# A Fourier-mixing and gated-MLP block in float32: a rebuilt opening, and sequence results gathered in DRAM

## The chip, the core and the metric

The kernel runs on one core of a Trainium2 chip. The metric is the device time of one execution in microseconds (us). The engines are TensorE (PE), VectorE (DVE), ScalarE (ACT), GpSimd (POOL) and SyncE (SP). Each works through its own instructions in the order in which the program lists them; between engines only semaphores order the work. SP, ACT and POOL can each issue DMA transfers, and an issue stands in its engine's order like any other instruction.

## The reference

```python
def _A_ref(x, dft_seq_re, dft_seq_im, dft_hid_re, dft_hid_im):
    a = jnp.einsum("bsd,ed->bse", x, dft_hid_re)
    b = jnp.einsum("bsd,ed->bse", x, dft_hid_im)
    return jnp.einsum("ts,bse->bte", dft_seq_re, a) - jnp.einsum("ts,bse->bte", dft_seq_im, b)

def _B_ref(x, w1, w3, w2):
    h = _silu(jnp.einsum("bsd,df->bsf", x, w1)) * jnp.einsum("bsd,df->bsf", x, w3)
    return jnp.einsum("bsf,fd->bsd", h, w2)

mod = (_silu(c) @ w_mod).reshape(c.shape[0], 6, 1, -1)
sa, ca, ga, sb, cb, gb = (mod[:, i] for i in range(6))
h = _layernorm(x, axis=-1) * (1 + ca) + sa
x = x + ga * _A_ref(h, ...)
h = _layernorm(x, axis=-1) * (1 + cb) + sb
x = x + gb * _B_ref(h, w1, w3, w2)
```

All is float32, with S = 2048 rows, D = 512 columns and F = 1792 hidden columns of the MLP. Each product is made of three matmuls, since each operand is split into a rounded high part and the rest.

## The kernel before, in words

A big tile is 128 partitions by 2 by 512 numbers; 50 slots of SBUF hold such tiles, and `take` and `give` hand slots out and back. PSUM has eight banks of 128 x 512.

**The opening** (up to 93 us). The symmetry of the Fourier matrices folds the 16 row blocks of x into eight pairs, `k` = 0 to 7: a block of rows and its mirror image. For a pair the kernel loads x (`load_x`; for `k` of 4 and more the mirror half by an indirect DMA on POOL, a gather), takes the layer norm's statistics (`norm_stats`, `norm_root`, `norm_inverse`, `norm_scale`), turns the rows on PE (`turn_rows`), applies the modulation (`modulate_rows`), forms sums and differences of the two halves (`mirror_sums`, tile `hs`), splits them (`sum_highs` to `hh` on ACT, `sum_lows` to `hl` on DVE) and multiplies by the hidden Fourier weights (`hid_product`, `hid_difference`, `hid_mirror`). The results are split again into the operands `uh`, `us` and `ul` of the sequence products. The hidden weights come in four parts `dt`, split by `w_highs` and `w_lows`; `differ_w` makes their differences `wd` on POOL.

The modulation's first two columns come from `wmr`: `mod_scale` scales rows of the matrix by `silu(c)`, `mod_sum` adds them over the partitions by matmuls against a column of ones, and reads the sums at once into `mod1`. `keep_warm` issues matmuls on a tile of ones whose result nobody reads.

The order of the rest of the opening isn't written out: `task` names each piece, its needs, a rank and its duration on each engine that can do it, `at` gives the time at which loads are expected, and `arrange` (lines 1283 to 1302) takes, among the pieces that could begin within 0.3 us of the earliest, the one of the lowest rank, and emits it. `PACE` and `RANK` set the ranks. `check_w` squares parts of the weights for a later test of their symmetry.

**The sequence products** (93 to 270 us). For each half `j` of the output tiles and each `k`, `seq_unit` runs two units `m` (real and imaginary) of 24 matmuls over all eight banks: `x` for e = 0 to 3 (16 matmuls), then `y` (8). So there are 32 units; those of the second half are called u0 to u15 here. Operands are loaded by `load_some` (two plain loads on SP and two gathers on POOL for a unit) and prepared by `prepare_some`, four units ahead. At the middle of a half (`turn`, k = 3) the x banks, and at its end (`end`, k = 7) x and y, are read out: DVE adds them, times the gate `ga`, to the residual tiles `xr`, which `load_xt` has loaded; at the end ACT copies x to two tiles `sum`, and `add_sums` adds these later to two tiles `xr`, on DVE.

**The second layer norm** (`ln2(t)` for the four row tiles `t`, in pairs (0, 2) and (1, 3)) runs in the background. `step` puts a function into a queue with its cost on DVE and ACT and the slots it needs; after each unit of PE work, `advance(dve, act)` adds credit and takes steps from the queue as long as credit and slots last:

```python
while queue and len(free) >= queue[0][0] + kept():
    _, *cost, fn = queue[0]
    if any(us > 0 and credit[n] <= 0 for n, us in enumerate(cost)):
        return
    queue.popleft()
    if fn is None:
        return
```

A step without a function (`pause`) so ends the call. After a sequence unit a call brings 2.2 us of DVE credit, 5.0 once no operands are left to prepare; there is no call after the units (k, m) = (3, 0) and (7, 0). `ln2` goes: sums over rows (`a1`, `a1b`, `rows`, `partition_sums`), mean (`a2`), centering (`a3`), squares (`a3b`, ACT), `keep` (writes `xr` to DRAM, where the MLP's results are later added), sums of squares (`a4`, `a1b`, `rows`, `partition_sums`), root (`a6`, ACT), inverse (`a6b`), scaling (`a7`), modulation (`a8`, ACT); then `chunk_parts` splits the result into `h2h` (ACT) and `h2l` (DVE). `drain` takes steps regardless of credit until what it asks for has been emitted.

**The MLP** (from 270 us): `up(0, 0)`, `up(1, 0)` (four blocks of 12 matmuls each), eight `down` units of 6 matmuls, then `judge` (the test of the symmetry), then `up(0, 2)`, which drains until `h2h` and `h2l` of tile 2 are emitted. Each block or unit is followed by `beside`, which spends its credit on weight jobs first and, if none are left, on the background. A down unit's result goes to `y` on ACT, and POOL adds y to the sums in DRAM by an accumulating DMA (line 1119).

Of the kernel before, what the change touches and what calls it, by code (L numbers as in the profile page):

```python
# [42 lines left out]
def folded(nc, pools, c, cp, wmr, wmc, x, xt, ctr, cti, wdr, wdi, w1, w3, w2, out):  # L43
# [156 lines left out]
    def load_x(k):  # L200
# [12 lines left out]
    def load_wm(v):  # L213
        for k in range(2):
            wm[v, k] = take(F32, "wmr")
            nc.sync.dma_start(wm[v, k], wmr[v, k])
# [5 lines left out]
    def load_hid(dt):  # L222
        i, par = HD[dt]
        raw_w[dt] = take(F32, "w")
        for m, w in enumerate((wdr, wdi)):
            for q in range(2):
                nc.sync.dma_start(raw_w[dt][q * 64 : (q + 1) * 64, m, :], w[i][par::2, q])

    nc.sync.dma_start(cc, cp)
    load_x(0)  # L230
    load_wm(1)
    load_wm(0)
    load_hid(0)
    load_x(1)
    for dt in range(1, ND):
        load_hid(dt)
# [26 lines left out]
    )  # L263
    first_tmp = take(F32, "tmp")
# [4 lines left out]
    def keep_warm(count):  # L269

        for _ in range(count):
            nc.tensor.matmul(warm, onesf[:, :P], onesf, start=True, stop=True)
# [15 lines left out]
    mod_acc = bank(6)  # L288
# [11 lines left out]
    def mod_sum(v):  # L300

        for dt in range(ND):
            nc.tensor.matmul(
                mod_acc[:, v * ND + dt : v * ND + dt + 1],
                hid_cols(wm[v, 0][:, 0, :], dt),
                onesf[:, :1],
                start=True,
                stop=True,
            )
        nc.vector.tensor_scalar(  # L310
            mod1[:, v, :], mod_acc[:, v * ND : (v + 1) * ND], float(v), None, op0=OP.add
        )
# [79 lines left out]
    def differ_w(dt):  # L392
# [5 lines left out]
        def pool(out, a, b, op):  # L398
            nc.gpsimd.tensor_tensor(out=out, in0=a, in1=b, op=op)

        if HD[dt][1]:
            pool(dd[:, 0, :], r[:, 0, 1, :], r[:, 0, 0, :], OP.add)
            pool(r[:, 1, 1, :], r[:, 1, 1, :], r[:, 1, 0, :], OP.add)
            nc.gpsimd.tensor_scalar(dd[:, 1, :], r[:, 1, 1, :], -1.0, None, op0=OP.mult)
        else:
            pool(dd[:, 0, :], r[:, 0, 1, :], r[:, 0, 0, :], OP.subtract)
            pool(dd[:, 1, :], r[:, 1, 0, :], r[:, 1, 1, :], OP.subtract)
# [89 lines left out]
    def sum_highs(k):  # L497
        hh[k] = take(F32R, "hh")
        copy(flat(hh[k]), flat(hs[k]))

    def sum_lows(k):
        hl[k] = take(F32R, "hl")
        minus(flat(hl[k]), flat(hs[k]), flat(hh[k]).bitcast(F32))
        give(hs.pop(k))
# [19 lines left out]
    def hid_product(k, dt):  # L524
        if dt == 0:

            hb[k] = bank(4 + k % 2)
            nc.tensor.matmul(
                hb[k], nought, flat(wt[0])[:, :N], start=True, stop=False, skip_group_check=True
            )  # L530
        for m in range(2):
            for n, (a, b) in enumerate(PASSES):
# [28 lines left out]
    def hid_mirror(k, high):  # L561

        h1b[k, high] = to = bank(6 + high)
        u = h1[k].rearrange("p a (d n) -> p a d n", d=ND)
# [59 lines left out]

    zero = take(F32, "zero")
# [73 lines left out]
    def seq_unit(n, m, between=None):  # L699
# [52 lines left out]
        if turn:  # L752
            for e in range(ND):
                residual(j + 2, e, acc["x", e], ga2)
        if end:
            part = [take(F32, "sum") for _ in range(2)]
            for e in range(ND):
                copy(part[e // 2][:, e % 2, :], acc["x", e])
                residual(j + 2, e, acc["y", e], ga)
            for i in range(2):  # L760
                for t in (j, j + 2):
                    step(background, 0, lambda i=i, t=t: add_sums(t, i, part[i]), 1.3)
                step(background, 0, lambda i=i: give(part[i]))

    def add_sums(t, i, src):
        for q in range(2):
            residual(t, 2 * i + q, src[:, q, :], ga)

    xr = {}

    def load_xt(t):
        xr[t] = [take(F32, "xr") for _ in range(2)]
        for i in range(2):
            nc.sync.dma_start(xr[t][i], xt[t, i])

    def residual(t, e, src, gate):
        xs = xr[t][e // 2][:, e % 2, :]
        nc.vector.scalar_tensor_tensor(
            xs, src, gate[:, e : e + 1], xs, op0=OP.mult, op1=OP.add
        )  # L780

# [6 lines left out]
    xc, sums = {}, {}  # L788

    def ln2(t):  # L790
# [84 lines left out]
        def keep():  # L875

            for i in range(2):
                sums[t, i] = dram.tile([P, 2, N], F32, name=f"sum_{t}_{i}")
                nc.sync.dma_start(sums[t, i], xr[t][i])
                give(xr[t][i])  # L880
            xr.pop(t)
# [8 lines left out]
        for slots, fn, dve, act in (  # L890
            (2, a1, 1.2, 0.0),
# [183 lines left out]

    def load_sums(t):
        xr[t] = [take(F32, "xr") for _ in range(2)]
        for i in range(2):
            nc.sync.dma_start(xr[t][i], sums[t, i])
# [202 lines left out]

    def arrange(hand_over=0.1, window=0.3):
        while pending:
# [14 lines left out]
            _, name, _, fn, ways = pending.pop(at)  # L1299
            ends[name] = (begin + us, engine)  # L1300
# [7 lines left out]
    def last_steps(k):  # L1308
# [3 lines left out]
        task(f"up{k}", r + RANK["up"], [f"diff{k}", f"odd{k}"], lambda: high_columns(k, 0), DVE=0.61)  # L1312
        task(f"ush{k}", r + RANK["ush"], [f"up{k}"], lambda: high_columns(k, 1), ACT=0.55)
        task(f"ulh{k}", r + RANK["ulh"], [f"ush{k}"], lambda: high_columns(k, 2), DVE=0.61)

    PACE = 7.15
    RANK = {
        "stats": -17,
        "root": -15,
        "inverse": -12,  # L1320
        "scale": -11.5,
        "turn": -11,
        "mod": -7,
        "sum": -11.5,
        "hh": -6.5,
        "hl": -9.7,
        "h1": -5,
        "prod": -2,
        "odd": -3,
        "mirror": 3,  # L1330
        "uh": 4,
        "us": 5,
        "ul": 6,
        "diff": 3.4,
        "up": 6,
        "ush": 12,
        "ulh": 6.6,
# [10 lines left out]
    nc.gpsimd.memset(flat(zero), 0.0)  # L1348
# [11 lines left out]
    at(13.6, "mod")  # L1360
    at(12.0, "turn0.0", "turn0.1")
    at(14.0, "x1")
    for dt in range(ND):
        at((12.1, 16.0, 18.0, 20.0)[dt], f"w{dt}")
    for k in range(2, 4):
        at(22.0 + 2.0 * (k - 2), f"x{k}")
    for engine in clear:
        clear[engine] = 13.6
# [3 lines left out]
    for dt in range(ND):  # L1372
        task(f"wh{dt}", -8 + 2 * dt, [f"w{dt}"], lambda dt=dt: w_highs(dt), ACT=0.8)
        task(f"wl{dt}", -7 + 2 * dt, [f"wh{dt}"], lambda dt=dt: w_lows(dt), DVE=0.8)
        task(f"wd{dt}", -6 + 2 * dt, [f"wl{dt}"], lambda dt=dt: differ_w(dt), POOL=3.0)
    for dt in range(2):
        task(f"wn{dt}", dt, [f"wl{dt}"], lambda dt=dt: w_minus(dt), ACT=1.0)
# [1052 lines left out]
```

## Time and profile before

| | us |
|---|---|
| Runs | 714.74 median of 3 (714.67 to 715.85) |
| Span of the profiled execution, first to last instruction | 715.7 |
| of it: opening, to the first sequence product | 93.1 |
| sequence products | 177.1 |
| MLP, to the last matmul | 437.3 |

The span begins at the first instruction, 0.24 us in the trace's time, and ends after the last store. Lines of a timeline give start, duration, engine, source line, operation, out<-in tiles with their shapes, and how often; in brackets the idle time before, and what ended it. A duration is from issue to the end of the pipeline, so that neighbours overlap. In a table by stretches each engine has its busy time and, in brackets, its instructions, in the order PE, PE's weight loads, DVE, ACT, POOL; then come the granted clock of TensorE (1.00 is full), the share of the DMA engines and GB/s.

### The profile page before, as it was taken

How to read it: one execution, taken by the hardware profiler on the slowest of the kernel's cores; microseconds unless marked ns; L12 is line 12 of the kernel's file. 1: busy time of each engine (PE TensorE's matmuls, PEld its weight loads, DVE VectorE, ACT ScalarE, POOL GpSimd, SP SyncE). 2: the span in 40 equal slices, each digit the busy share in tenths (PEclk: the TensorE clock that was granted, in tenths of full speed). 3: DMA queues.
4: the chain of work that ended last, by engine and by line, in shares of the span. 5: the costliest groups of instructions: out<-in, count | busy, mean ns of one | idle time of the engine just before them, and what ended most of it. 6: DMA issues, size and time to landing. Idle time of an engine off the chain costs nothing.

```text
span 715.7 us, 8791 instructions
## 1 busy us (share of the span) xinstructions
PE 689.8 (96%) x3094; PEld 563.4 (79%) x3094; DVE 551.9 (77%) x873; ACT 428.7 (60%) x700; POOL 129.8 (18%) x147
## 2 busy tenths in 40 slices
PE   7699999999999999999999999999999999999995
PEld 3587888888888888777888788787788888888784
DVE  4889887999899977679997887897666456664663
ACT  4687975455453665646677767667665655656420
POOL 3520073443435000100100101011010101101000
PEclk8599999999999999999999999999999999999998
DMA  8630089878588530442667566376854748447503
GB/s 245 225 116 3 5 289 355 280 257 294 172 312 266 171 142 31 75 76 86 130 164 161 133 148 137 69 127 136 266 115 91 154 76 182 87 91 129 165 1 122
DMA packets 37956, 108.93 MB, mean 152 GB/s; under 512 B 4880, under 2 KB 5136, under 8 KB 37904
## 3 DMA queue, kind: packets, MB, share of 16 engines
q0 software_dynamic: 12352, 43.00, 28.8%
q1 hardware_dynamic: 25552, 65.29, 27.7%
q8 instruction: 26, 0.43, 0.2%
q14 instruction: 26, 0.21, 0.1%
HBM read 76.81 MB, written 33.55 MB: 154 GB/s over the span
## 4 chain that ended last, share of the span: by engine, by line
PE 60%; issue 23%; DVE 6%; DMA 4%; ACT 4%; POOL 2%; SPq 1%; POOLq 0%; ACTq 0%; DVEq 0%
PE bank L100 32%; PE bank L723 25%; POOL sum L1119 2%; PE bank L533 2%; DMA sum<-y 2%; DMA x<-in_x 1%; PE bank L569 1%; DMA wmr<-in_wmr 1%; DVE hl L90 1%; ACT hm L485 1%; PE bank L469 1%; DVE hs L90 1%; ACT y L317 0%; DVE hm L487 0%; ACT ho L87 0%
## 5 line engine op out<-in xcount | busy, mean ns | idle before, releaser
L100 PE MATMUL bank<-hf,w2h 128*128 128x512 f32 (+1 forms) x452 | 140.8, 391 | 1.0 <-ACT y L317 0.7
L1119 POOL DMA_DIRECT2D sum<-y x48 | 41.1, 856 | 390.9 <-ACT y L317 373.1
L100 PEld LDWEIGHTS bank<-hf,w2h 128*128 128x128 f32 x452 | 84.3, 188 | 22.8 <-DVE hf L90 3.4
L100 PE MATMUL bank<-hf,w2l 128*128 128x512 f32 (+1 forms) x226 | 87.6, 388 | 0.0
L317 ACT ACTIVATE y<-bank,gb 128x512 f32<-128x512 f32 x96 | 65.0, 683 | 19.1 <-PE bank L100 18.4
L87 ACT ACTIVATE hf<-v 128x512 fp32r<-128x512 f32 x56 | 35.3, 630 | 67.2 <-DVE v L96 62.6
L93 DVE TENSOR_TENSOR v<-bank,x 128x512 f32<-128x512 f32 x36 | 24.7, 686 | 34.8 <-PE bank L100 34.8
L170 POOL DMA_INDIRECT re<-in_ctr,mirror x32 | 36.5, 1142 | 73.8 <-PE bank L569 37.6
L723 PE MATMUL bank<-bh,us 128*128 128x512 f32 x128 | 49.9, 390 | 0.0
L723 PE MATMUL bank<-bh,ul 128*128 128x512 f32 x128 | 49.8, 389 | 0.0
L723 PE MATMUL bank<-d,us 128*128 128x512 f32 x128 | 49.8, 389 | 0.0
L723 PE MATMUL bank<-d,uh 128*128 128x512 f32 x128 | 49.8, 389 | 0.0
L723 PE MATMUL bank<-l,us 128*128 128x512 f32 x128 | 49.8, 389 | 0.0
L723 PE MATMUL bank<-l,uh 128*128 128x512 f32 x128 | 49.8, 389 | 0.0
L93 DVE TENSOR_TENSOR x<-bank,x 128x512 f32<-128x512 f32 x36 | 24.8, 688 | 32.4 <-PE bank L100 28.7
L100 PEld LDWEIGHTS bank<-hf,w2l 128*128 128x128 f32 x226 | 42.4, 188 | 8.4
L90 DVE TENSOR_TENSOR hf<-v,hf 128x512 fp32r<-128x512 f32 x56 | 38.5, 687 | 12.2 <-ACT hf L87 12.1
L1197 ACT ACTIVATE v<-v 128x512 f32<-128x512 f32 x36 | 22.8, 632 | 38.9 <-DVE v L93 38.9
L87 ACT ACTIVATE x<-bank 128x512 f32<-128x512 f32 x72 | 41.4, 587 | 7.1 <-PE bank L100 6.5
L170 POOL DMA_INDIRECT im<-in_cti,mirror x32 | 35.1, 1096 | 34.4 <-DVE l L90 9.7
L100 PE MATMUL bank<-h2h,w1h 128*128 128x512 f32 x80 | 31.8, 397 | 1.5 <-ACT h2h L87 1.5
L100 PE MATMUL bank<-h2l,w1h 128*128 128x512 f32 x80 | 32.0, 400 | 0.8 <-DVE h2l L90 0.8
(243 smaller groups left out, 1785.7 us busy)
## 6 DMA issues: line engine op xcount, KB each, us to landing
sum<-y POOLq DMA_DIRECT2D x48, 512.0 KB, 5.4
w<-in_w SPq DMA_DIRECT2D x42, 512.0 KB, 4.5
re<-in_ctr SPq DMA_DIRECT2D x32, 256.0 KB, 5.5
im<-in_cti SPq DMA_DIRECT2D x32, 256.0 KB, 4.9
wmc<-in_wmc SPq DMA_DIRECT2D x8, 512.0 KB, 6.9
xr<-in_xt SPq DMA_DIRECT2D x8, 512.0 KB, 7.6
sum<-xr SPq DMA_DIRECT2D x8, 512.0 KB, 6.6
x<-in_x SPq DMA_DIRECT2D x12, 256.0 KB, 4.5
```

The lines of the kernel that those rows point to most:

```text
L87: nc.scalar.activation(dst, src, AF.Copy, scale=scale)
L90: nc.vector.tensor_tensor(out=dst, in0=a, in1=b, op=OP.subtract)
L93: nc.vector.tensor_tensor(out=dst, in0=a, in1=b, op=OP.add)
L100: nc.tensor.matmul(acc, lhs[a], rhs[b], start=first and n == 0, stop=last and n == len(PASSES) - 1, skip_group_check=more,)
L170: nc.gpsimd.indirect_dma_start(dst, None, rows, bass.IndirectOffsetOnAxis(ap=at, axis=0))
L317: nc.scalar.activation(dst, src, AF.Identity, scale=by)
L469: nc.tensor.transpose(turned[k][dt // 2][:, at : at + P], hid_cols(xz[k][:, side, :], dt), anti if side and where(k)[1] else ident,)
L485: nc.scalar.activation(dst, src, AF.Identity, bias=sa, scale=ca1)
L533: nc.tensor.matmul(halves(hb[k])[:, m, :], sides((hh, hl)[a][k])[:, dt, m, :], wu[dt][:, b, m, :], start=False, stop=dt % 2 == 1 and n == ...
L723: nc.tensor.matmul(acc[what, e], lhs, rhs, start=begin and i == 0, stop=(end or (turn and what == "x")) and i == len(terms) - 1, skip_grou ...
L1119: nc.gpsimd.dma_start(sums[t, d // 2], y, accum_op=OP.add)
L1197: behind(k != 0 or q == 0, lambda: nc.scalar.activation(v, src, AF.Silu))
```

## The change

In the opening: part of the first loads are issued by ACT; the last `wmr` tile comes in two halves; the sums over partitions are 128 columns wide in banks of their own, and reading them is a step apart (`mod_read`); `hid_begin` and six narrow warming matmuls stand between; `differ_w` is on DVE; a gather of x waits, by a copy of one number on POOL, for `wd[0]`; pair 0's split and products go in halves; `arrange` fills PE's planned idle time with narrow warming matmuls until the first `hid_mirror`; ranks, durations and load times are new.

In the sequence products: `begin_sums` copies x from DRAM to the DRAM sums; `move` reads the banks out, times the gate, by ACT (at the end of the second half y by DVE) into tiles that POOL adds to the DRAM sums; `ln2` begins with `load_sums` and four pauses; `load_xt`, `residual`, `add_sums` and the store in `keep` go.

```diff
+    def load_x(k, other=nc.sync):
+        if k >= NK // 2:
+            nc.gpsimd.tensor_copy(held, wd[0][0:1, 1, 0:1].bitcast(F32))
...
-            nc.sync.dma_start(xz[k][:, 1, :], x[NK - 1 - i][1::2])
+            other.dma_start(xz[k][:, 1, :], x[NK - 1 - i][1::2])
...
+    def load_wm(v, k, queue):
+        wm[v, k] = take(F32, "wmr")
+        for n in range(2) if (v, k) == (0, 1) else (slice(0, 2),):
+            queue.dma_start(wm[v, k][:, n], wmr[v, k, :, n])
...
-    load_x(0)
-    load_wm(1)
-    load_wm(0)
-    load_hid(0)
+    load_x(0, nc.scalar)
+    load_wm(1, 0, nc.scalar)
+    load_wm(1, 1, nc.sync)
+    load_wm(0, 0, nc.scalar)
+    load_wm(0, 1, nc.sync)
+    for dt in range(2):
+        load_hid(dt, nc.sync)
     load_x(1)
...
-                mod_acc[:, v * ND + dt : v * ND + dt + 1],
+                mod_acc[v][:, cols(dt)],
                 hid_cols(wm[v, 0][:, 0, :], dt),
-                onesf[:, :1],
+                onesf[:, :P],
...
         if HD[dt][1]:
-            pool(dd[:, 0, :], r[:, 0, 1, :], r[:, 0, 0, :], OP.add)
...
+            plus(dd[:, 0, :], r[:, 0, 1, :], r[:, 0, 0, :])
+            nc.vector.scalar_tensor_tensor(
+                dd[:, 1, :], r[:, 1, 1, :], -1.0, r[:, 1, 0, :], op0=OP.mult, op1=OP.subtract
+            )
...
         if turn:
-            for e in range(ND):
-                residual(j + 2, e, acc["x", e], ga2)
+            move({(j + 2,): "x"}, ga2)
         if end:
...
+            move({(j, j + 2): "x", (j + 2,): "y"}, ga, j == 1)
...
+    def move(what, gate, both=False):
+
+        parts = {}
+        for i in range(2):
+            for to, name in what.items():
+                parts[to, i] = take(F32, "sum")
+            for q in range(2):
+                for to, name in what.items():
+                    dst, e = parts[to, i][:, q, :], 2 * i + q
+                    if both and name == "y":
+                        nc.vector.tensor_scalar(
+                            dst, acc[name, e], gate[:, e : e + 1], None, op0=OP.mult
+                        )
+                    else:
+                        copy_by(dst, acc[name, e], gate[:, e : e + 1])
+        for to in what:
             for i in range(2):
...
+                for t in to:
+                    nc.gpsimd.dma_start(sums[t, i], parts[to, i], accum_op=OP.add)
+                moved.append([3, parts[to, i]])
...
+    def begin_sums(t):
+        for i in range(2):
+            sums[t, i] = dram.tile([P, 2, N], F32, name=f"sum_{t}_{i}")
+            nc.sync.dma_start(sums[t, i], xt[t, i])
...
         for slots, fn, dve, act in (
+            (4, lambda: load_sums(t), 0.0, 0.0),
+            *[pause] * 4,
             (2, a1, 1.2, 0.0),
...
+            if engine == "PE" and filling:
+
+                keep_warm(max(0, int((begin - clear["PE"] - 0.1) / 0.23)), P)
...
-    PACE = 7.15
+    PACE = 7.39
...
-    for v in (1, 0):
-        for h in range(2):
-            mod_scale(v, h)
+    keep_warm(1)
+    for v, h in ((1, 0), (1, 1), (0, 0)):
+        mod_scale(v, h)
+    mod_sum(1)
+    copy(nought, zero[:, 0, :P])
     clear_z()
-    for v in (1, 0):
-        mod_sum(v)
-        keep_warm(2 if v else 1)
-    give(first_tmp)
...
+    hid_begin(0)
+    keep_warm(6, P)
+    mod_scale(0, 1)
+    mod_read(1)
+    mod_sum(0)
+    mod_read(0)
...
-        if k == 2:
-            load_xt(j + 2)
-        if k == 5:
-            load_xt(j)
+        if k == 1:
+            begin_sums(j + 2)
+        if k == 4:
+            begin_sums(j)
```

More of the change, by code (lines that the diff above doesn't have):

```diff
@@ L309, in mod_sum, with mod_read @@
             )
-        nc.vector.tensor_scalar(
-            mod1[:, v, :], mod_acc[:, v * ND : (v + 1) * ND], float(v), None, op0=OP.add
-        )
+    def mod_read(v):
+        for at in (slice(0, ND),) if v else [slice(dt, dt + 1) for dt in range(ND)]:
+            nc.vector.tensor_scalar(
+                mod1[:, v, at],
+                mod_acc[v][:, ::P][:, at],
+                float(v),
+                None,
+                op0=OP.add,
+            )
         for h in range(2):
@@ L522, in halves, with hid_begin, hid_product @@
         return b.rearrange("p (a n) -> p a n", a=2)
[L524 to L532, printed above, removed]
+    def hid_begin(k):
+        hb[k] = bank(4 + k % 2)
+        nc.tensor.matmul(
+            hb[k], nought, flat(wt[0] if k else zz)[:, :N], start=True, stop=False, skip_group_check=True
+        )
+    def hid_product(k, dt, ms=range(2), ns=range(3)):
+        if dt == 0 and k:
+            hid_begin(k)
+        for m in ms:
+            for n in ns:
+                a, b = PASSES[n]
                 nc.tensor.matmul(
@@ L772, in load_xt, with return_moved, load_sums @@
+    def return_moved():
+        for at in moved:
+            at[0] -= 1
+        while moved and moved[0][0] < 0:
+            give(moved.popleft()[1])
+    def begin_sums(t):
+        for i in range(2):
+            sums[t, i] = dram.tile([P, 2, N], F32, name=f"sum_{t}_{i}")
+            nc.sync.dma_start(sums[t, i], xt[t, i])
+    def load_sums(t):
         xr[t] = [take(F32, "xr") for _ in range(2)]
         for i in range(2):
[L774 to L780, printed above, removed]
+            nc.sync.dma_start(xr[t][i], sums[t, i])
@@ L875, in keep @@
         def keep():
[L877 to L881, printed above, removed]
+            for x in xr.pop(t):
+                give(x)
         def a9():
@@ L1504, in folded @@
     give(zz)
+    while moved:
+        behind(6, lambda t=moved.popleft()[1]: give(t))
     USED = {"w1": (0.0, 0.5), "w3": (1.2, 0.5), "y": (0.0, 0.6), "own": (0.7, 0.0)}
```

194 lines of the change are left out of this document (101 added, 93 removed).

## The prediction, made before the changed kernel was run

> **What bounds the kernel now.** The page comes first: the span, the engines' shares, the prices of a scaled copy on ACT and of an accumulating transfer.
>
> ```profile
> span 715.7 us, 8791 instructions
> PE 689.8 (96%) x3094; PEld 563.4 (79%) x3094; DVE 551.9 (77%) x873; ACT 428.7 (60%) x700; POOL 129.8 (18%) x147
> L317 ACT ACTIVATE y<-bank,gb 128x512 f32<-128x512 f32 x96 | 65.0, 683 | 19.1 <-PE bank L100 18.4
> L1119 POOL DMA_DIRECT2D sum<-y x48 | 41.1, 856 | 390.9 <-ACT y L317 373.1
> sum<-y POOLq DMA_DIRECT2D x48, 512.0 KB, 5.4
> ```
>
> TensorE is busy 96% of the span, so time is won or lost only where it idles or runs slowly. The busy time by stage (stretch, its length, then each engine's busy time) shows where that is.
>
> ```profile
> 13.30:18.80 5.50, 5.50 (x14) 3.43 (x15) 1.65 (x5) 0.83 (x2) 3.56 (x4) 0.50 0.98 246
> 18.80:36.00 17.20, 11.68 (x42) 9.23 (x42) 15.11 (x33) 12.73 (x24) 10.01 (x11) 0.50 0.69 222
> 36.00:40.00 4.00, 4.00 (x25) 3.54 (x24) 2.48 (x4) 3.12 (x8) 0.00 (x0) 0.99 0.00 0
> 40.00:93.10 53.10, 51.02 (x336) 45.06 (x335) 48.78 (x91) 44.79 (x90) 8.42 (x7) 1.00 0.19 56
> 93.10:270.20 177.10, 177.10 (x786) 146.69 (x785) 158.92 (x223) 95.72 (x185) 63.54 (x61) 1.00 0.75 252
> 302.90:310.00 7.10, 4.81 (x14) 3.54 (x14) 4.55 (x14) 4.41 (x6) 1.89 (x3) 0.76 1.01 181
> ```
>
> From 93.1 to 270.2 (the sequence products) TensorE never idles at full clock: nothing can be won there. The opening runs at half clock (0.50) up to 36 us. From 40 on three engines are near full at once: PE 96%, DVE 92%, ACT 84%. The other hole is the 7.1 us at 302.9. The timeline names the opening's events.
>
> ```profile
> 2.54 2.24 SPq L216 DMA_DIRECT2D wmr<-in_wmr  x4
> 13.22 1.54 DVE L296 SCALAR_TENSOR_TENSOR wmr<-wmr,sc,wmr 128x512 f32<-128x512 f32 x2 [0.79 <-DMA wmr<-in_wmr]
> 13.30 3.76 PE L272 MATMUL bank<-tmp 128*128 128x512 f32 x4
> 18.60 0.16 DVE L310 TENSOR_SCALAR mod<-bank 128x4 f32<-128x4 f32 x1 [3.77 <-PE bank L303]
> 18.80 0.54 DVE L487 TENSOR_SCALAR hm<-bank,mod 128x256 f32<-128x256 f32 x1
> 19.09 1.24 SPq L227 DMA_DIRECT2D w<-in_wdi  x2
> 24.07 0.80 PE L533 MATMUL bank<-wu,hh 128*128 128x256 f32 x2 [3.16 <-ACT hh L87]
> 93.08 0.40 PE L723 MATMUL bank<-bh,us 128*128 128x512 f32 x1
> ```
>
> The modulation sums could be read at about 15, but two warming calls (3.76 us) stand before them; hidden products begin at 24.07, sequence products at 93.08.
>
> **The opening.** Four edits have one answer: the earlier wm loads, the warming regrouped around wide column sums, `differ_w` moved from POOL to DVE, the new order. First the start. Three transfers fewer stand ahead of the last wm tile on SP (0.56 us of issue each), and it comes in two pieces; but all share the DMA engines, so I take 1.2 us off the 14.76 at which its scaling now ends and not 1.7, then add 0.7 for sums and reads: modulation starts at 14.3 instead of 18.80. Bounds: 13.3 if loads are quicker still, 18.8 if the six narrow warming matmuls delay the sums as the wide ones do.
>
> Then the work from there to 93.1. DVE has 15.11 + 2.48 + 48.78 = 66.4 us, ACT 12.73 + 3.12 + 44.79 = 60.6: 127.0 in 74.3 us, 85% of two engines. What changes in it:
>
> ```profile
> L399 POOL TENSOR_TENSOR wd<-w 128x256 fp32r<-128x256 f32 x6 | 5.8, 989 | 11.2 <-DMA w<-in_wdr 11.2
> L90 DVE TENSOR_TENSOR wu<-w,wu 128x256 fp32r<-128x256 f32 x2 | 1.4, 686 | 0.0
> L90 DVE TENSOR_TENSOR wu<-w,wu 128x256 fp32r<-128x256 f32 x2 | 0.8, 422 | 0.0
> L188 ACT ACTIVATE junk<-wd 128x512 f32<-128x512 f32 x4 | 2.6, 640 | 0.0
> ```
>
> The two `wu` rows are the same operation while POOL computes `wd` (19 to 27 us) and after (27 to 40). So `differ_w` on DVE adds 8 x 0.422 = 3.4 and ends an interference of 4 x 0.26 = 1.1 in these rows; the four checks (2.6) get ranks behind all else and fill gaps. 127.0 + 3.4 - 1.1 - 2.6 = 126.7, as before. At the old 85% it ends at 14.3 + 74.3 = 88.6, at 100% at 77.7. TensorE's floor is between: 11.68 at half clock is 5.8 at full, plus 4.0 and 51.0, 60.9; begun some 3 us after the modulation, 14.3 + 3 + 60.9 = 78.2. I take 92%, DVE's own share from 40 on, for both, because modulation and scaling may go to either: 126.7 / (2 x 0.92) = 68.9, so sequence products begin at 83.2: **-9.9 us** (ends: -4.5 and -13.5, the latter 1.4 above TensorE's floor). Held gathers and the split sums of block 0 are inside this term: the gathers wait for `wd` on POOL already, through its in-order queue.
>
> The clock needs a look. In 13.30 to 18.80 TensorE shows 5.50 of 5.50 busy, and the clock stays at 0.50 to 36. The Trainium skill (TensorE: Matmul & The Clock Gate, "What's actually happening") says that about 3.4 us of sustained activity releases a throttle that is the default. Row and rule disagree, unless the one-column sums in that stretch do not count as activity; the wide sums would then release the clock by about 18, which is the 92% case. By the row alone it stays at half to 36, which is the second rival.
>
> **Results taken out by ScalarE.** DVE loses 12 reads of banks and 16 additions over both halves, all under 100% TensorE: worth nothing. ACT gets eight copies at the end of the first half, in the order x0, y0, x1, y1. They can't pass y0, whose products end 1.4 us before the unit does (177.1 us for 32 units is 5.5 each, 0.23 for each of its 24 products, and six follow y0's); six copies of 0.683 later, 4.1, x3 is out, 2.7 us into the next unit, which reaches x3 after 2.7: 0 to 0.7, taken 0. POOL's eight accumulating DMAs (5.4 us to landing) stand ahead of gathers, behind operands prepared four units ahead: nothing.
>
> The Trainium skill (SBUF — State Buffer, "SBUF: two separate sides") says that a DMA issued from GpSimd can't have its descriptors written while DVE holds the shared port in a two-port mode. DVE is 90% busy here (158.92 of 177.10), so this speaks against the accumulation; by it each waits for one DVE operation, an estimate of 8 x 1.2 = 10 us over 90 us of POOL's queue, and the sum stays.
>
> **The second layer norm is what this costs.** Its background steps are spent by credit: a call after each sequence unit (u0 to u15 of the second half, none after u6 and u14), one after each of the eight up blocks (B1 to B8, from 270.2), one after each of eight down units (D1 to D8, from 291.98). A PAUSE ends its call. Before, tile 0 adds up to u4 and is done after u13; tile 2 follows at once:
>
> ```profile
> 262.24 1.22 DVE L93 TENSOR_TENSOR t<-xr,xr 128x1024 f32<-128x1024 f32 x1
> 288.48 0.69 DVE L93 TENSOR_TENSOR t<-t 128x512 f32<-128x512 f32 x1
> 291.87 0.25 DVE L813 TENSOR_REDUCE s<-q 32x16 f32<-32x64 f32 x1
> 294.92 0.31 ACT L853 ACTIVATE s<-s,eps 32x16 f32<-32x16 f32 x1
> 295.26 0.24 DVE L856 RECIPROCAL s<-s 32x16 f32<-32x16 f32 x1 [0.93 <-ACT s L853]
> 297.02 2.36 DVE L96 TENSOR_TENSOR xc<-xc,stat 128x1024 f32<-128x1024 f32 x2
> 298.33 1.52 ACT L867 ACTIVATE xc<-xc,sb,cb 128x512 f32<-128x512 f32 x2 [1.37 <-issue]
> 291.98 0.62 PE L100 MATMUL bank<-hf,w2h 128*128 128x512 f32 x2
> 302.63 0.39 PE L100 MATMUL bank<-hf,w2l 128*128 128x512 f32 x1
> 303.45 1.05 ACT L87 ACTIVATE h2h<-xc 128x1024 fp32r<-128x1024 f32 x1
> 304.56 0.50 PE L100 MATMUL bank<-h2h,w1h 128*128 128x512 f32 x1 [1.53 <-ACT h2h L87]
> 305.81 0.79 PE L100 MATMUL bank<-h2l,w1h 128*128 128x512 f32 x1 [0.76 <-DVE h2l L90]
> 309.95 0.39 PE L100 MATMUL bank<-h2h,w3h 128*128 128x512 f32 x1
> 307.58 0.42 DVE L979 TENSOR_REDUCE sq<-chk 128x8 f32<-128x256 f32 x1 [0.30 <-POOL sq L978]
> 310.54 0.14 DVE L999 TENSOR_SCALAR bad<-fine 1x1 int32<-1x1 f32 x1
> ```
>
> Tile 2 is barely ready when the third up block wants it: 1.53 us of wait, 0.76 more. After, the queue loses four steps of 1.3 and gets a load and four pauses for each tile. Tile 0's load is issued after u2, its first sum after u7 instead of u4; once nothing is left to prepare, calls bring 5.0 instead of 2.2, and its last low part comes after u15, with tile 2's load. Tile 2's pauses take u15, B1, B2, B3; then a1 after B4, a1b and rows B6, the sums B7, the mean B8, a3(0) D1, the squares D2 and D4, a4 D5, a1b D6, rows D7, the sums D8. That is where B7 stood before, at 291. The drain before the third up block emits all the rest at once.
>
> Times from there. D4 ends at 291.98 + 4 x 1.36 = 297.4; its copy and the second square (ACT in order, 0.7 + 1.05 and some queueing) end at 299.9; a4 1.2; a1b to sums 3.0 (288.48 to 292.12, less 0.6 of other work): 304.1, root 304.5. `judge` now stands ahead on DVE: 3.1 us (307.58 to 310.68), not before POOL is past the last accumulation at about 305: 308.1. Then reciprocal and spread 1.8, first product 1.2, the pairs on ACT 2 x 1.5, high part 1.05: 315.2 against 304.5 now, 10.7 later; a colder clock after it 0.7 more (from 305.81 to 309.95 the old stall takes 4.1 for 2.5 us of products). At u15 the low part of tile 0 falls behind the last bank reads on DVE: 0 to 1.2, taken 0.4. Together **+11.8** (8.3 without `judge`, 13.5 if POOL is later). ln2 of tiles 1 and 3 loses four additions and gains eight pauses that fall on idle calls; it meets its point at about 450 as before: 0.
>
> **Sum.** Span 715.7 - 9.9 + 11.8 = 717.6. The runs' median is 714.74 (714.67 to 715.85), 1.0 under the profiled span, so **716.6**, 0.3% slower. What a measurement of this kernel can tell from no change is 0.2%, 1.4 us.
>
> **Rivals.** *The opening wins more than the stall costs.* One mechanism: clock and vector engines hold 95% from 14.3 on, so sequence products begin at about 80 (-13.1) while the stall takes its lower end (+8.3): 709.9. It decides from the point where they begin before 81.3 (93.1 - 11.8). For it: PE, DVE and ACT reach 96, 92 and 84% from 40 on already. Against: weights are still being issued at 19 to 20 us, and three full engines wait for each other.
>
> *The clock stays at half in the lead-in*, 85% as before: -4.5 + 11.8, 722.0. For it: 5.5 busy us that released nothing. Against: the pieces that fill gaps.
>
> *POOL is late*: accumulations hold up gathers, and a sequence unit waits; six of 0.86 us behind eight copies of 0.68 hold the queue for 10.6 us. Against: four units (22 us) are prepared ahead. Held 25 us, by DMA engines that are 75% busy, the next unit is 3 late: 719.7.
>
> *The layer norm isn't late*, because DVE, relieved, catches up: 714.74 - 9.9 + 0.4 = 705.2. Against: the place in the order is given by calls, not by DVE's load.
>
> **How the numbers follow.** Forecast 0.48 (0.30 slower by over 0.2%, 0.15 within, 0.03 faster), opening wins 0.22, half clock 0.17, POOL 0.08, not late 0.05. Faster 0.03 + 0.22 + 0.05 = 0.30, same 0.15, slower 0.30 + 0.17 + 0.08 = 0.55. The forecast's own range is 713 to 720; taken to the first two rivals, 709.5 to 722.5, which leaves out the last and tails.
>
> **What would show it.** The first sequence product at 83 (80 to 89); clock 1.00 from about 18; `hm` at 14.3. In the PE waits one of about 11 us on `h2h` ahead of the third up block, `judge` ahead of the reciprocal. Sequence products still without a gap. Wrong would be a short wait there, or a start before 81.

## The result and the profile after

The changed kernel takes 728.62 us (median of 5 runs, 726.22 to 729.02) against 714.74 (714.39 to 715.85): a ratio of 1.018, 95% interval 1.0162 to 1.0198. It is 1.8% slower; the forecast was 716.6 us, 0.3% slower, with a range to 722.5. Both kernels were profiled once more later, and e1 (below) is the new opening alone. The stages of the five profiles, from the first matmul of each on TensorE's timeline:

| us | before (shown) | before again | after (shown) | after again | e1 |
|---|---|---|---|---|---|
| opening, to the first sequence product | 93.08 | 91.67 | 84.48 | 85.19 | 84.74 |
| sequence products | 177.14 | 177.15 | 182.55 | 184.17 | 177.10 |
| `up(0, 0)` to the start of the last down product | 32.41 | 32.41 | 33.72 | 33.73 | 32.41 |
| from there to `w3` of the third up block | 7.32 | 5.97 | 18.93 | 18.82 | 5.99 |
| rest | 405.75 | 405.70 | 404.72 | 404.59 | 404.76 |
| span | 715.7 | 712.9 | 724.4 | 726.5 | 705.0 |
| time of that execution | not known | 714.77 | 726.22 | 728.27 | 706.82 |

A run takes 1.7 to 2.4 us more than its span wherever both are known. So the profile shown of before is of an execution of some 717.5 us, an estimate; the fair base is the second one. Against it the changed kernel as shown gains 7.2 us in the opening and 1.0 in the rest, and loses 5.4 in the sequence products, 1.3 at the first up block and 13.0 at the third: 11.5 us. The second profile of after has the time of its session's median (728.27) and loses 7.0 in the sequence products.

The page of the profile after, first its shares, then its DMA issues (size of each, median us to landing):

```profile
span 724.4 us, 8924 instructions
PE 688.4 (95%) x3152; PEld 564.9 (78%) x3152; DVE 530.3 (73%) x849; ACT 438.7 (61%) x721; POOL 133.8 (18%) x157
sum<-y POOLq DMA_DIRECT2D x48, 512.0 KB, 5.4
re<-in_ctr SPq DMA_DIRECT2D x32, 256.0 KB, 7.7
sum<-sum POOLq DMA_DIRECT2D x16, 512.0 KB, 9.6
```

VectorE is relieved by 21.6 us (551.9 to 530.3) and nothing comes of it. The new accumulations take 9.6 us to land, not the 5.4 of the old ones. What TensorE waits for (in all, times, longest):

```profile
PE bank L100 <- ACT h2h L87: 12.6, 1, 12.6
PE bank L750 <- ACT sum L335: 3.6, 1, 3.6
PE bank L100 <- DVE h2l L90: 1.5, 2, 1.0
```

The first row is the forecast's; the second wasn't forecast. Its story begins 45 us earlier, on POOL, at the end of the first half. The timeline of after:

```profile
173.92 1.91 POOL L805 DMA_DIRECT2D sum<-sum  x2 [7.82 <-ACT sum L335]
176.22 1.73 POOL L805 DMA_DIRECT2D sum<-sum  x2 [0.39 <-ACT sum L335]
184.42 0.85 POOL L805 DMA_DIRECT2D sum<-sum  x1 [6.47 <-DMA sum<-sum]
191.33 0.85 POOL L805 DMA_DIRECT2D sum<-sum  x1 [6.05 <-issue]
192.48 1.08 POOL L170 DMA_INDIRECT re<-in_ctr,mirror  x1 [0.30 <-issue]
202.55 0.69 DVE L90 TENSOR_TENSOR l<-re 128x512 fp32r<-128x512 f32 x1 [11.89 <-DMA re<-in_ctr,mirror]
204.90 0.63 ACT L188 ACTIVATE re<-l 128x512 f32<-128x512 f32 x1 [15.70 <-DVE d L93]
221.85 2.40 ACT L335 ACTIVATE sum<-bank,ga 128x512 f32<-128x512 f32 x4
222.57 0.50 PE L750 MATMUL bank<-bh,us 128*128 128x512 f32 x1 [3.56 <-ACT sum L335]
```

POOL issues four accumulations of x, then stops: the accumulation of y goes into a tile of DRAM that one of x is still being added to, and waits for it, 6.47 us. The next one waits 6.05; its row names no releaser, but the trace fits the same cause: the two accumulations of x into these two tiles land at 184.14 and 190.83, 0.3 and 0.5 us before y's are issued. The next gather is issued at 192.48, 14.5 us after the last of x, its operand reaches VectorE after 11.89 us of idleness, and ScalarE after 15.70. The four units prepared ahead are used up; from then on preparation trails, until at the turn of the second half ScalarE takes the banks out only at 221.85, behind a square of an operand for the test of the symmetry, and TensorE stands 3.56 us and then runs at half clock for a while. Busy time by stretch:

```profile
174.00:200.00 26.00, 26.00 (x116) 21.55 (x115) 12.02 (x15) 10.10 (x21) 11.14 (x12) 1.00 0.99 246
222.00:232.00 10.00, 9.43 (x34) 7.58 (x35) 8.82 (x13) 6.41 (x13) 6.88 (x7) 0.83 1.03 270
16.20:84.50 68.30, 64.78 (x444) 58.63 (x444) 63.69 (x131) 63.88 (x131) 13.01 (x15) 1.00 0.34 101
```

While POOL stands still TensorE notices nothing (26.00 of 26.00): the loss appears at 219, some 40 us after POOL's first wait began. From 222 the clock is at 0.83 over ten us, worth 1.7; with the 3.56 that is 5.3 of the 5.4. The third row answers to the opening's forecast.

The third up block went as the prediction's row of steps said:

```profile
297.55 1.23 DVE L93 TENSOR_TENSOR t<-sq,sq 128x1024 f32<-128x1024 f32 x1 [2.09 <-ACT sq L884]
303.18 0.31 ACT L892 ACTIVATE s<-s,eps 32x16 f32<-32x16 f32 x1
303.74 0.42 DVE L1017 TENSOR_REDUCE sq<-chk 128x8 f32<-128x256 f32 x1 [1.76 <-POOL sq L1016]
306.76 0.23 DVE L895 RECIPROCAL s<-s 32x16 f32<-32x16 f32 x1
312.66 1.99 ACT L87 ACTIVATE h2h<-xc 128x1024 fp32r<-128x1024 f32 x2
313.75 0.80 PE L100 MATMUL bank<-h2h,w1h 128*128 128x512 f32 x1 [12.61 <-ACT h2h L87]
319.68 0.39 PE L100 MATMUL bank<-h2h,w3h 128*128 128x512 f32 x1
```

The squares are added at 297.55, the root is at 303.18, the test (`judge`, L1017) stands ahead of the reciprocal, and the first product comes at 313.75.

### The profile page after: what moved, and what is told of

Same layout as the page of the kernel before. It is cut to its first block, busy times and chain, and to the rows that moved or that the text cites. A ratio compares the mean times of both kernels' runs of the same rounds, so it can differ in the third digit from the quotient of the medians.

```text
span 724.4 us, 8924 instructions
## 1 busy us (share of the span) xinstructions
PE 688.4 (95%) x3152; PEld 564.9 (78%) x3152; DVE 530.3 (73%) x849; ACT 438.7 (61%) x721; POOL 133.8 (18%) x157
## 4 chain that ended last, share of the span: by engine, by line
PE 63%; issue 11%; DVE 8%; DMA 8%; ACT 6%; POOL 2%; SPq 1%; POOLq 0%; ACTq 0%; DVEq 0%
PE bank L100 47%; PE bank L750 12%; DMA sum<-sum 3%; DMA im<-in_cti,mirror 2%; PE bank L559 1%; DMA wmr<-in_wmr 1%; PE bank L598 1%; DMA sum<-y 1%; ACT xc L906 1%; POOL im L170 1%; DVE xc L96 1%; POOL re L170 1%; SPq L231 1%; ACT hf L87 1%; PE bank L576 1%
## 5 line engine op out<-in xcount | busy, mean ns | idle before, releaser
L335 ACT ACTIVATE y<-bank,gb 128x512 f32<-128x512 f32 x96 | 65.4, 684 | 21.6 <-PE bank L100 21.4
L1230 ACT ACTIVATE v<-v 128x512 f32<-128x512 f32 x36 | 22.8, 632 | 35.6 <-DVE v L93 35.6
L100 PE MATMUL bank<-h2h,w1h 128*128 128x512 f32 x80 | 32.3, 403 | 12.6 <-ACT h2h L87 12.6
L170 POOL DMA_INDIRECT im<-in_cti,mirror x32 | 33.0, 1031 | 23.7 <-issue 6.7
```

Of the source, the lines that this page charges most:

```text
L100: nc.tensor.matmul(acc, lhs[a], rhs[b], start=first and n == 0, stop=last and n == len(PASSES) - 1, skip_group_check=more,)
L170: nc.gpsimd.indirect_dma_start(dst, None, rows, bass.IndirectOffsetOnAxis(ap=at, axis=0))
L335: nc.scalar.activation(dst, src, AF.Identity, scale=by)
L1230: behind(k != 0 or q == 0, lambda: nc.scalar.activation(v, src, AF.Silu))
```

## The experiments

**One part alone.** e1 undoes the change in the sequence products (old `residual`, `add_sums`, `load_xt`, `keep`, no pauses); e2 undoes the opening.

> The new opening with the old way of taking out the sequence results. Theory 'POOL is late' (the sequence products lost 5.4 us, in the profile of the changed kernel, to accumulating DMAs in front of the gathers): none are there now, so the sequence products take 177 us again, the third up block waits 1.5 us as before, and the time is 714.7 - 8.6 = 706 us. Rival 'the new opening hands operands over late': the sequence products still take 182 us, 711 us. If the opening's gain is given back later, 714.

Measured: 708.13 us against 716.44 of before in the same session, ratio 0.9892 (0.9869 to 0.9916). Opening 84.74, sequence products 177.10, the third up block as before. The opening alone is a gain of 1.1%, and in this profile it gives nothing back (others do lose something at the start of the sequence products, see "After again").

> The old opening with the new way of taking out the sequence results. If the two parts add up: sequence products 182 us, 12.6 us of wait before the third up block, 728.6 + 8.6 = 737 us. Rival (the loss in the sequence stage comes from both together): sequence products 177 us, 727 us.

Measured: 735.06 us, ratio 1.0269 (1.0238 to 1.0299); opening 92.49, sequence products 181.92, 13.4 us of wait before the third up block. The parts add up roughly: -8.3 and +18.6 make +10.3, against +12.6 to 13.9 for both. The loss comes with the results' new way.

**The accumulations.** e3 issues the same transfers, two of them later:

```diff
-        for to in what:
+        for to, name in what.items():
             for i in range(2):
-                for t in to:
-                    nc.gpsimd.dma_start(sums[t, i], parts[to, i], accum_op=OP.add)
-                moved.append([3, parts[to, i]])
+                if name == "y" and not both:
+                    put_later.append([4, lambda to=to, i=i: put(to, i)])
+                else:
+                    put(to, i)
```

> The changed kernel, but the two accumulating DMAs of y at the end of the first half are issued four units later, behind the gathers. The same transfers and the same bytes. Theory 'POOL is late': the waits of 6.5 and 6.0 us on POOL ahead of the gathers go, VectorE's wait of 11.9 us goes, the sequence products take 177 to 178 us: 728.6 - 5 = 723 us. Rival 'the DMA engines are full' (share 1.05 at 186 to 200 us): the gathers land as late as before, sequence products 182 us, 728 us.

Measured: 722.39 us, 1.009 (1.0067 to 1.0114), 6.2 us below the changed kernel; sequence products 177.61. The timeline of e3:

```profile
176.60 1.73 POOL L804 DMA_DIRECT2D sum<-sum  x2 [0.39 <-ACT sum L335]
178.63 1.08 POOL L170 DMA_INDIRECT re<-in_ctr,mirror  x1 [0.30 <-DMA re<-in_ctr]
192.59 0.94 POOL L170 DMA_INDIRECT im<-in_cti,mirror  x1 [2.21 <-issue]
193.53 1.93 POOL L804 DMA_DIRECT2D sum<-sum  x2
193.09 0.69 DVE L90 TENSOR_TENSOR l<-re 128x512 fp32r<-128x512 f32 x1 [2.06 <-DMA re<-in_ctr,mirror]
194.22 1.23 DVE L93 TENSOR_TENSOR d<-re,re 128x1024 fp32r<-128x1024 f32 x1 [0.45 <-DMA re<-in_ctr,mirror]
```

The first gather goes out at 178.63, right behind the accumulations of x; eight are issued before y's two, which now find their predecessors landed and go in 1.93 us without a wait. VectorE idles 2.06 us where it idled 11.89. The bytes are the same, so it was the order on POOL and not the DMA engines. The rule that the prediction cited from the Trainium skill (SBUF — State Buffer, "SBUF: two separate sides") is about a two-port mode of VectorE. VectorE works at 193.09 and 194.22 and the two issues run through; but no row shows that these two operations hold the port in such a mode, so the rule isn't tested here, and a VectorE that is 90% busy was no measure of it.

**The layer norm.** e4 takes tile 2's pauses away by loading earlier, and e6 moves the test:

```diff
+            *[(4, lambda: load_sums(t), 0.0, 0.0), *[pause] * 4] * (t != PAIRS[0][1]),
...
             (0, keep, 0.0, 0.0),
+            *[(4, lambda: load_sums(2), 0.0, 0.0)] * (t == PAIRS[0][0]),
```

> The changed kernel, but the load of tile 2's sums is issued with tile 0's steps and tile 2 has no pauses of its own. Theory 'the pauses push the second layer norm of tile 2 behind': the wait before the third up block falls from 12.6 us to between 0 and 2, the time to 728.6 - 11.5 = 717 us. Rival 'the steps are late through VectorE or ScalarE, not through the calls': the wait stays above 8 us, 725 us.

Measured: 721.32 us, 1.0085 (1.0055 to 1.0114). That is 7.3 us less, not 11.5. The third block's stage falls from 18.93 to 12.25: 4.5 us of wait on `h2h` are left, and then 2.4 on `h2l`, for now the test stands ahead of `h2l`. Tile 0 is still three units later than before, and so is all behind it.

```diff
-    judge()
     up(0, 2)
+    judge()
```

> The changed kernel, but the test of the symmetry is moved behind the third pair of up blocks. The forecast put 3.1 us of the wait before that block down to it (reciprocal behind the test on VectorE): the wait on h2h falls from 12.6 to 9.5 us, 728.6 - 3.1 = 725.5 us. Rival: the test only fills time in which VectorE would wait for the root (303.49) anyway: 728 us.

Measured: 725.65 us, 1.0146 (1.0119 to 1.0172); the wait on `h2h` is 9.4 us. The test's 3.1 us were sized rightly, but half of it comes back in the trace: the test now stands among the pair sums on VectorE, and behind the block TensorE waits 1.9 us, 0.5 before, for a bank that ScalarE copies.

> The changed kernel with three mends: the accumulating DMAs of y four units later (as in e3), tile 2's load without pauses of its own (as in e4), and the test of the symmetry behind the third pair of up blocks, not ahead of it. If the losses are those two and add up: 728.6 - 6.2 - 7.3 - 2.4 (the wait on h2l that e4 still had behind the test) = 712.7 us. Rival 'the results by ScalarE cost nothing in themselves': then 708, as with the new opening alone. Rival 'the mends get in each other's way': above 716.

Measured: 717.34 us, 1.0037 (1.0019 to 1.0056). Expected too low: against e1 the profile still loses 5.0 us at the third up block, 1.7 behind it (the test again), 1.6 in the sequence products and 1.3 at the first up block.

e11 gives tile 0 two pauses in place of four, so that its first sum stands after u4 as before; the test is where it was.

> The changed kernel with the accumulating DMAs of y four units later (e3), tile 2's load with tile 0's steps (e4), and two pauses in place of four behind tile 0's load, so that tile 0's first sum comes after u4 as before. Theory 'the layer norm is late by calls alone': the wait before the third up block is 1.5 us as before, from the last down unit to the block's w3 6 us in place of 18.9, the whole 709 to 710 us, 1 to 2 above e1. Rival 'VectorE or ScalarE is late for its own reasons': the wait of 4.5 us of e4 stays, 714 us.

Measured: 719.69 us, 1.0059 (1.0042 to 1.0076). The half of it on the layer norm is right to the hundredth: 5.97 us to the third `w3`, as in before again, 32.42 to the last down product. But the sequence products take 188.39. The timeline of e11:

```profile
190.98 2.04 SPq L834 DMA_DIRECT2D xr<-sum  x2
213.82 1.23 DVE L93 TENSOR_TENSOR t<-xr,xr 128x1024 f32<-128x1024 f32 x1 [5.22 <-DMA xr<-sum]
228.90 0.80 PE L750 MATMUL bank<-bh,us 128*128 128x512 f32 x1 [7.74 <-ACT sum L335]
```

The load is issued at 190.98 and is there at 213.8. The sum that needs it stands in VectorE's order among the preparations of operands and holds them for 5.22 us; TensorE pays 7.74 at the same place as after, and a cold clock behind it. So the pauses are no oversight: they cover the way back from DRAM, which before didn't exist. With them the layer norm is late, without them the operands are.

**The opening's parts**, each undone in e1. e7 leaves out the narrow matmuls that `arrange` puts into planned idle time; e8 computes the differences of the weights on POOL; e14 has the old `PACE` and `RANK`; e15 has no `held` copies.

> e1 (new opening alone, 708.1 us, first sequence product at 84.7) without the 50 and more narrow warming matmuls that fill TensorE's planned idle time. Theory 'the fillers hold the clock': TensorE is idle from 16.2 to 22.2, the clock falls to 0.50 there and comes back only after some us of unbroken work; the first sequence product is at 87 to 89, 711 us. Rival 'the wide sums release it and that is enough, VectorE and ScalarE set the pace': 84.7, 708 us.

> e1 with the differences of the hidden weights back on POOL (in the planner too). The forecast counted 3.4 us more on VectorE and 1.1 us less interference for the move to VectorE; by that, undoing it gives 2.3 us of VectorE's time back: the first sequence product at 83.5, 707 us. Rival 'POOL's 12 us of differences and the gathers behind them are late': 86 to 88, 710 us.

> e1 (708.1 us, first sequence product at 84.7) with the old PACE and RANK, all else of the opening new. If the searched order is what raises the use of VectorE and ScalarE from 85 to 92%: first sequence product at 88, 711 us or more. Rival 'the differences on VectorE (4.7 us, e8) and the fillers (2.2 us, e7) are all of it': 85 to 86, 709 us.

> e1 without the copies on POOL that hold the gathers of x until the weights' first difference is there. If holding keeps the DMA engines (share 1.0 and more until 17 us) free for the weights: without it four gathers of 256 KB go out from about 10 us, the weights come some 3 us later, first sequence product at 86 to 88, 710 us. Rival 'the hold does nothing': 84.7, 708 us.

| | us | ratio (95%) | first sequence product |
|---|---|---|---|
| e1 | 708.13 | 0.9892 (0.9869 to 0.9916) | 84.74 |
| e7, no fillers | 712.28 | 0.9956 (0.9942 to 0.997) | 86.92 |
| e8, differences on POOL | 713.2 | 0.9968 (0.9951 to 0.9986) | 89.41 |
| e14, old order | 712.65 | 0.9964 (0.9946 to 0.9982) | 88.33 |
| e15, gathers not held | 712.26 | 0.9949 (0.9933 to 0.9965) | 87.74 |

Each part alone is worth 4 us or more; 2.2 + 4.7 + 3.6 + 3.0 exceeds the whole gain, so they hang together: with one of them undone the order no longer fits the rest. e8's expectation was wrong in sign; POOL takes 1.9 to 3.1 us for each of the four differences, one after the other until 22.9, and that these are on the way to the operands is likely but not shown. In e15 the four gathers stand ahead of the weights, and the modulation begins late. Its first row in the timeline of e15:

```profile
18.95 1.02 ACT L499 ACTIVATE hm<-bank,mod 128x256 f32<-128x256 f32 x2 [1.22 <-DVE mod L322]
```

And in that of e1, 2.5 us earlier:

```profile
16.41 1.02 ACT L501 ACTIVATE hm<-bank,mod 128x256 f32<-128x256 f32 x2 [1.89 <-DVE mod L324]
```

**The clock.** e9 puts wide sums into the kernel before; e10 is the kernel before itself.

> The kernel before with one thing changed: the modulation's sums are 128 columns wide in two banks of their own, in place of one column. In the profile of before TensorE is busy without a break from 11.82 to 20.9 us and the clock stays at 0.50 until 36. Theory 'one-column matmuls do not count as activity': with wide sums in their place the clock is back at 1.00 by 19 us; the lead-in's hidden products are at full speed, but it drops again in the idle time after 20.9, so the first sequence product is only 0 to 3 us earlier (90 to 93), 712 to 715 us. Rival 'the clock does not see the width': 0.50 until 36 as before, 93.1, 715 us.

> The kernel before, unchanged. The forecast took the runs to be 1.0 us under the profiled span (714.74 against 715.7). In the changed kernel the runs are 1.8 to 2.2 us over their spans. If that is so here too, the span of this profile is about 713, and the profile shown of before was of one of the slower executions; which stage is shorter shows where executions differ. Rival: span 715.7 and time 714.7 again.

e9: 714.34 us, 0.9977 (0.9964 to 0.9991), first sequence product at 91.07. It doesn't decide: the clock was at 1.00 there until 20 us, so nothing was to be released. e10: 715.42 us, span 712.9 in a run of 714.77: the profile shown of before was one of the slower executions, as was expected. Its opening is 1.4 us longer and its third up block too, and the clock is what differs. The stretches in which it changes (the last three figures are clock, DMA share and GB/s), first in the profile shown of before:

```profile
12.00:12.25 0.25, 0.25 (x4) 0.25 (x4) 0.25 (x1) 0.25 (x1) 0.00 (x0) 0.81 1.02 238
36.00:37.00 1.00, 1.00 (x6) 0.84 (x5) 0.98 (x1) 0.44 (x2) 0.00 (x0) 0.98 0.00 0
```

In before again, with two stretches between the changes:

```profile
9.00:12.00 3.00, 1.80 (x8) 1.43 (x8) 1.93 (x3) 2.45 (x5) 0.00 (x0) 0.56 1.05 348
12.77:16.18 3.41, 3.41 (x10) 2.38 (x11) 2.21 (x4) 0.83 (x2) 2.01 (x3) 0.50 1.08 257
16.18:19.59 3.41, 3.41 (x11) 2.38 (x11) 0.16 (x1) 0.00 (x0) 1.92 (x4) 0.50 0.98 246
28.00:30.00 2.00, 2.00 (x12) 2.00 (x11) 1.93 (x7) 0.87 (x2) 1.70 (x2) 0.54 0.97 381
```

In e7:

```profile
19.00:20.00 1.00, 0.00 (x0) 0.00 (x0) 0.96 (x4) 1.00 (x3) 0.00 (x0) 0.97 0.88 221
26.00:28.00 2.00, 2.00 (x10) 1.64 (x9) 1.97 (x4) 0.37 (x1) 1.84 (x2) 0.81 0.75 281
```

In e1:

```profile
9.25:9.50 0.25, 0.25 (x3) 0.25 (x3) 0.00 (x0) 0.25 (x1) 0.00 (x0) 0.72 1.03 393
12.75:13.00 0.25, 0.25 (x4) 0.25 (x3) 0.21 (x2) 0.00 (x0) 0.00 (x0) 0.96 1.13 279
```

A mean of 0.81 over 0.25 us is 0.62 of it at 1.00: so the clock falls at 12.16 in before and comes back at 36.04, at 9.36 and 29.84 in before again, at 19.94 and 26.76 in e7, at 9.36 and 12.77 in e1. The clock was low for 23.88, 20.48, 6.82 and 3.41 us: 7, 6, 2 and 1 times 3.41. The Trainium skill (TensorE: Matmul & The Clock Gate, "What's actually happening") gives a free-running window of 3413 ns, whose place differs from run to run; these rows agree. In e7 TensorE is idle from 15.8 to 21.83 for want of fillers and pays two windows at half clock. What runs in the two windows from 12.77 of before again, in which it never idles, is in its timeline:

```profile
12.38 1.87 PE L303 MATMUL bank<-tmp,wmr 128*128 128x1 f32 x8 [1.54 <-DVE wmr L296]
14.11 3.76 PE L272 MATMUL bank<-tmp 128*128 128x512 f32 x4
17.67 1.71 PE L303 MATMUL bank<-tmp,wmr 128*128 128x1 f32 x8
```

Each has some 1.3 to 1.7 us of one-column matmuls in it.

**After again.**

> The changed kernel, unchanged. Its profiled run took 726.22 us, the median 728.62: 2.4 us lie in no stage seen so far. Theory 'they are in the sequence stage, whose gathers come late by an amount that differs from run to run': opening 84 to 85, up blocks to third w3 52.6 as before, and sequence products 183 to 185 us where the profile is of a slower run. Rival 'the clock in the lead-in': the first sequence product later than 84.5.

728.27 us, 1.0173 (1.0149 to 1.0196), and the profiled run is the one of the median. The 2.05 us between it and the first profile's run are 1.6 in the sequence products (184.17) and 0.7 in the opening, where the clock has a mean of 0.57 from 72 to 76, less 0.2 elsewhere. So the 184 came, but not for the reason expected: the 1.6 us lie at the start of the products, 42 us before the first accumulation is issued (133.67). The timeline of after again:

```profile
90.72 0.69 DVE L93 TENSOR_TENSOR ho<-bank,ho 128x512 f32<-128x512 f32 x1 [4.27 <-remote]
91.46 0.50 PE L750 MATMUL bank<-d,us 128*128 128x512 f32 x1 [1.50 <-DVE ho L93]
```

VectorE reads a bank of the last hidden products, and TensorE waits 1.50 us for the result. The matmuls that fill this bank are recorded as over at 88.1, but TensorE's signal comes only at 90.69; in the profile shown of after VectorE begins at 87.45, as soon as they end. Why the signal is late no run shows. Seven of the thirteen profiles with the new opening have this wait, of 0.6 to 1.6 us (e5, e6, e7, e11, e12, e15 and this one), and none of the four with the old. In these seven the opening does hand an operand over late, as e1's rival had it, though by a small part of what it gains.

**A better kernel.** e12 takes e1 and moves the modulation of tile 2 to VectorE:

```diff
+                if t == PAIRS[0][1]:
+                    xs = xc[t, i][:, q, :]
+                    nc.vector.tensor_scalar(
+                        xs, xs, cb1[:, e : e + 1], sb[:, e : e + 1], op0=OP.mult, op1=OP.add
+                    )
+                    continue
```

> e1 (708.1 us) with the modulation of tile 2's second layer norm (four scalings of 128x512) on VectorE, which is idle from 291.0 to 296.2 there, in place of ScalarE, where it stands between the copies of the down units' results. If the wait before the third up block in e1 (1.5 and 0.8 us, and a colder clock) comes from ScalarE's queue: from the last down unit to w3 3 to 4 us in place of 6.0, 705.5 us. Rival: the root at 286.5 sets the end anyway, 708 us.

707.58 us, 0.9891 (0.9874 to 0.9909). The third block's stage is 4.80 in place of 5.99, less than was hoped for; the profile loses 1.6 us to the wait just described, and the time isn't told from e1's. e1 and e12 are both faster than the kernel before and the changed one.

## Why the prediction was wrong

**The step that failed** is the sentence "POOL's eight accumulating DMAs (5.4 us to landing) stand ahead of gathers, behind operands prepared four units ahead: nothing". It counted the issues and one landing. That a second accumulation into the same tile waits on POOL for the first to land, twice and one after the other, was not in it. It cost 5.4 us in the shown profile and 5.5 in the one of median time (7.0 less the 1.5 at the start of the products, which isn't POOL's); with the two issued later 4.9 of the 5.4 go in the profile, and 6.2 between the medians (e3). The rival "POOL is late" had the cover right (22 us, used up) and the price too small at 3 us: it counted the late unit, not what comes behind it, the banks read late at the turn and the clock that falls there. It was taken as an alternative, where it came on top.

**The opening**: -9.9 forecast, -8.6 against the profile it was reckoned from, -7.2 against the other. The work was sized rightly: 63.69 + 63.88 us on VectorE and ScalarE, 127.6 against 126.7 forecast, in 68.3 us, 93% where 92% was taken. The start was not: the last scaling ended at 14.4, not 13.6, and the reads took until 16.18, with `hm` there and not at 14.3. The rival "the opening wins more" has a slip in its sum: 95% from 14.3 on gives 14.3 + 126.7 / (2 x 0.95) = 81.0, not about 80, and so 710.9, not 709.9. The clock was as the 92% case wanted it, though less through the wide sums than through fillers: without them it falls (e7). That one-column matmuls don't count, the forecast's guess, has the two windows of before again for it: TensorE busy for 3.41 of 3.41, one-column matmuls among them, the clock still 0.50; in e1 one window without them, of transposes and wide matmuls, released it. In e2, which has the opening of before, one window busy throughout with only some 0.6 us of one-column matmuls in it (14.70 to 18.12) released it too, so that it may be their share that matters. e9 couldn't test it, so it stays likely and not shown.

**The layer norm**: +11.8 forecast. The order of events was the forecast's, and from the first up product to the end of the first high part it took 46.6 us (313.66 less 267.03), 1.3 of them the stall at the first block, where 45.0 and a stall of 0.4 were forecast (315.2 less 270.2). Against the profile it was reckoned from the third block's stage is 11.6 longer, forecast 11.4; the stall at the first block was mis-sized, 1.3 for 0.4. Against the fair base the stage is 13.0 longer, since there the clock stays at 1.00 (300 to 310). e11 shows that the place in the order of calls is the cause: with the calls as before the stage is as before.

**The sum.** "1.0 under the profiled span" compared a median with the span of an execution that was not among its runs. Base and conversion were both wrong and cancel: 712.9 - 9.9 + 11.8 + 1.8 is again 716.6. With the sizes measured in the profile of median time it is 712.9 - 6.5 (opening) + 7.0 (sequence products) + 14.2 (both blocks) - 1.1 (rest) + 1.8 = 728.3. So of the 11.7 us that were missed POOL has 5.5, the late bank at the start of the products 1.5, the opening 3.4 and the layer norm 2.4 (of each of these two 1.4 are the clock of the profile from which they were reckoned), and the rest, where the changed opening gains 1.0 to 1.1 us that were not followed up, -1.1. The late bank stays open, and so does that gain.

**Results taken out by ScalarE** were rightly put at nothing by themselves: e3 has them, and 177.61 us of sequence products, 0.5 more than e1. That a relieved VectorE doesn't bring the layer norm forward was right too.

## What to carry to other kernels

A transfer that must wait for an earlier one into the same place holds everything behind it in its queue: before adding one, ask what it waits for, and put it behind the loads that the next stage needs. A round trip through DRAM needs time that someone has to cover; the pauses that cover it delay all later work in the same order. And compare a time with a span of the same execution only.

## What wasn't expected of the hardware

Landing times grew with the company: an accumulation of 512 KB took 5.4 us to land in the MLP, and the four of x at the end of the first half, beside gathers, 7.5 to 14.1. Part of that is their own company: the four at the end of the second half, with no gather about, took 5.4 to 11.3. Two loads of the sums took 22.8 us in e11, at a DMA share near 1. And two executions of one program differ by the clock: the kernel before gets it back at 36.04 or at 29.84 us, and has a window at half clock at the third up block or none; its other stages agree to 0.05 us.
